# Keys in four loads, another order of the head, group 1's work between the first products, sums between the elu halves

## Chip, cores, metric

One core of one Trainium2 chip. The metric is device microseconds of the whole program. A "ratio" below is the mean time of one kernel's fast runs over that of the kernel before in the same rounds, with a 95% interval; it is not quite the ratio of the medians that are quoted beside it.

## The reference, cut

```python
# attention: batch 4, heads 4, seq 1088, head_dim 32, r 8
a, b = x @ S1.T, x @ S2.T                  # phi(x): outer product of a and b, 64 features
kv  = einsum('bhsf,bhsd->bhfd', phi(k), v);  z = sum(phi(k), seq)
x   = (phi(q) @ kv) / (phi(q) . z + 1e-6)  # -> (4352, 128)
# feed forward: w_in (128, 2048), w_out (2048, 128), both float64 in memory
h = x @ w_in;  g = where(h > 0, h, exp(min(h, 0)) - 1);  out = g @ w_out
```

## The kernel before, the parts that matter

Tokens go in 9 groups of 512 (the last of 256), d_ff in 8 pairs of 256 columns. A step is one pair of one group: `mm1` (two products h with w_in), `elu` (two ScalarE and one VectorE instruction for each half c, giving gg), and two steps later `mm2` (two products o with w_out, accumulated over a segment of pairs); `fin1` takes the accumulated o out of PSUM. Weights arrive as float64 and are rounded to fp32 on the chip, by `RA`, `RB` (ScalarE), `RC` (c, d, e), one pair at a time between about 10 and 60 us.

```python
    def round_e(raw, dst, pool=False):
        mant = raw[:, :, 0].bitcast(F32)
        if pool:                                   # pairs 4 to 7
            nc.gpsimd.tensor_mul(mant, mant, _ap(tiny[:], [[0, dst.shape[1]]]))
            nc.gpsimd.tensor_mul(dst, mant, dst)
        else:
            nc.vector.scalar_tensor_tensor(dst, mant, 2.0 ** -20, dst, op0=MUL, op1=MUL)
    ...
    load_hd(nc.sync, "k", k, 0, 0, KT)             # KT = 9 of 17 tiles of 32 floats: runs of 1152 bytes
    load_hd(nc.scalar, "k", k, 0, KT, NT)          # runs of 1024 bytes
    ...
    load_hd(nc.sync, "q", q, 0, 0, 8)
    load_w(0, 0);  load_v(nc.sync, 0);  load_w(1, 0);  load_w(1, 1);  load_w(0, 1)
    load_hd(nc.sync, "q", q, 0, 8, NT)
    ...                                            # the head (cut)
    keep_warm(2)                                   # filler products for TensorE
    transp(kT, "k", 0, 0, KT);  transp(kT, "k", 0, KT, NT)
    KF(0, 0);  transp(qT, "q", 0, 0, 8);  q1_first();  KO(0, 0);  KF(0, 1);  KF(0, 2);  q2_first()
    RA(0);  RB(0);  KO(0, 1);  KO(0, 2);  RA(1);  RA(2)
    KA(0, 0);  q4_first();  make_SX();  KA(0, 1);  RB(1);  RB(2);  KA(0, 2)
    transp(qT, "q", 0, 8, NT);  q5_first()
    mm1(0, 0)
    ...                                            # rounding of pair 1, then group 1: q2(1), mm1(0, 1), q4(1), q5(1)
    for n in range(N + 4):                         # the steps
        ...                                        # mm1, extras
        if 2 <= n < N:
            elu(g, cp)                             # both halves
        ...
        if 2 <= n < N + 2:
            mm2(...)
            if last:
                fin1(...)
```

KF makes the key features (abp), KO their outer product (kp), KA the products with v (kv), make_SX a small constant product (SX), q1 to q5 the same chain for the queries of a group.

## Time and profile before

| | |
|---|---|
| median (runs) | 303.12 us (302.9 to 303.38) |
| span of the profiled run | 300.9 us |
| busy: TensorE, VectorE, ScalarE, GpSimd | 96%, 56%, 62%, 6% |
| first product with w_in / products without holes / product o after the rounding | 20.19 / 28.41 / 63.61 us |

Shares of the whole span hide the stages: TensorE is nearly always full, so the questions are when the unbroken stream of h and o begins and which holes it has. The prediction shows the lines. In a timeline line the first number is the start in us, the second the length, and the bracket the idle time before it with its releaser.

### The profile page before, as it was taken

The page shows a single profiled execution, that of the slowest core. Times are in us where ns is not written, and L with a number is a line of the kernel's source. Part 1 is how long each engine was busy: PE and PEld are TensorE (multiplying, and loading weights), DVE is VectorE, ACT ScalarE, POOL GpSimd, SP SyncE. Part 2 cuts the span into 40 slices and gives each one's busy share as a digit, 9 for nine tenths or more (in the row PEclk, how much of TensorE's full clock was granted, in tenths as well). Part 3 has the DMA queues.
Part 4 walks back from the last instruction along what each step waited for, and adds up shares of the span by engine and source line. Part 5 has one row for each costly group of instructions (what it writes and reads, how often), then busy time and mean ns, then how long its engine had stood idle before and what let it go on. Part 6 is the DMA issues. An engine that isn't in the chain of part 4 may idle for free.

```text
span 300.9 us, 4049 instructions
## 1 busy us (share of the span) xinstructions
PE 290.1 (96%) x1454; PEld 147.7 (49%) x1454; DVE 169.7 (56%) x297; ACT 187.8 (62%) x354; POOL 17.1 (6%) x45
## 2 busy tenths in 40 slices
PE   8987999999999999999999999999999999999994
PEld 5863344644444455444544464445444444444682
DVE  5788899963745565536344656426443644354441
ACT  1526896565666645746775656656774687568682
POOL 2010023440000000100000000100000000000000
PEclk9999999999999999999999999999999999999999
DMA  6932998320010100001001100001001000110020
GB/s 187 338 118 74 200 216 201 48 74 0 9 28 9 27 2 0 2 9 27 2 1 17 18 2 0 0 14 23 0 0 23 16 0 1 15 22 0 3 33 17
DMA packets 38291, 13.37 MB, mean 44 GB/s; under 512 B 32768, under 2 KB 36480, under 8 KB 38272
## 3 DMA queue, kind: packets, MB, share of 16 engines
q1 hardware_dynamic: 37984, 12.86, 19.0%
q10 hardware_dynamic: 288, 0.26, 0.3%
q8 instruction: 11, 0.18, 0.2%
q14 instruction: 8, 0.07, 0.1%
HBM read 10.88 MB, written 2.23 MB: 44 GB/s over the span
## 4 chain that ended last, share of the span: by engine, by line
PE 83%; DVE 8%; ACT 3%; DMA 2%; issue 2%; SPq 1%; DVEq 0%
PE o L522 36%; PE h L493 34%; PE xps L472 3%; PE kv L293 3%; PE qtp L457 2%; PE abwp L360 2%; DMA v<-in_v_dram 2%; DVE gg L508 1%; ACT e L502 1%; PE abp L266 1%; ACT e L501 1%; DVE kT L247 1%; DVE kp L253 1%; DVE W L114 1%; PE x0ps L424 1%
## 5 line engine op out<-in xcount | busy, mean ns | idle before, releaser
L508 DVE SCALAR_TENSOR_TENSOR gg<-e,h 128x512 f32<-128x512 f32 (+1 forms) x144 | 93.0, 654 | 98.3 <-ACT e L502 97.8
L522 PE MATMUL o<-gg,W 128*128 128x512 f32 (+1 forms) x288 | 131.1, 578 | 1.2 <-ACT oT L535 0.7
L493 PE MATMUL h<-xg,W 128*128 128x512 f32 (+1 forms) x288 | 128.8, 569 | 1.8 <-DVE xg L484 0.7
L501 ACT ACTIVATE e<-h 128x512 f32<-128x512 f32 (+1 forms) x144 | 81.4, 565 | 26.1 <-PE h L493 25.7
L502 ACT ACTIVATE e<-e 128x512 f32<-128x512 f32 (+1 forms) x144 | 87.3, 606 | 4.6
L493 PEld LDWEIGHTS h<-xg,W 128*128 128x128 f32 x288 | 54.5, 190 | 65.2 <-issue 55.2
L522 PEld LDWEIGHTS o<-gg,W 128*128 128x128 f32 x288 | 51.9, 190 | 51.4 <-issue 43.7
L270 ACT COPY ab<-abp 128x256 f32<-128x256 f32 (+1 forms) x12 | 3.7, 317 | 25.0 <-PE abp L266 25.0
L365 ACT COPY abw<-abwp 128x384 f32<-128x384 f32 (+1 forms) x8 | 3.7, 458 | 22.9 <-PE abwp L360 22.9
L253 DVE TENSOR_TENSOR kp<-ab 128x1024 f32<-128x1024 f32 (+1 forms) x12 | 12.2, 1022 | 8.4 <-ACT ab L270 8.2
L458 ACT COPY qpT<-qtp 128x512 f32<-128x512 f32 (+1 forms) x16 | 8.3, 561 | 12.6 <-PE qtp L457 12.6
L293 PEld LDWEIGHTS kv<-v,kp 128*64 128x64 f32 (+1 forms) x288 | 9.5, 139 | 7.5 <-DVE gg L508 5.3
L293 PE MATMUL kv<-v,kp 128*64 128x33 f32 (+3 forms) x288 | 10.8, 226 | 0.3 <-DMA v<-in_v_dram 0.3
L381 DVE TENSOR_TENSOR qp<-an,abw 128x1024 f32<-128x1024 f32 (+1 forms) x8 | 9.3, 1159 | 0.3
L472 PE MATMUL xps<-qpT,kvS 64*32 64x128 f32 (+2 forms) x200 | 8.7, 298 | 0.3 <-ACT qpT L458 0.3
L483 ACT COPY xg<-xps 128x256 f32<-128x256 f32 (+1 forms) x8 | 2.9, 359 | 9.8 <-PE xps L472 9.8
L457 PEld LDWEIGHTS qtp<-ident,qp 128*128 128x128 f32 x60 | 6.8, 140 | 4.4 <-issue 4.0
L457 PE MATMUL qtp<-ident,qp 128*128 128x128 f32 x60 | 8.2, 277 | 0.6 <-DVE qp L381 0.6
L313 POOL TENSOR_TENSOR zm<-kvz,zmask 128x32 f32<-128x32 f32 x3 | 0.7, 241 | 126.0 <-ACT kvz L307 126.0
L266 PE MATMUL abp<-Sab,kT 128*64 128x64 f32 x136 | 7.4, 249 | 0.5 <-DVE kT L247 0.5
L360 PEld LDWEIGHTS abwp<-SW,qT 128*64 128x64 f32 x120 | 5.2, 136 | 5.4 <-issue 5.3
L266 PEld LDWEIGHTS abp<-Sab,kT 128*64 128x64 f32 x136 | 6.1, 159 | 3.6 <-issue 2.9
(84 smaller groups left out, 126.2 us busy)
## 6 DMA issues: line engine op xcount, KB each, us to landing
raw<-in_moe_w_in_dram SPq DMA_DIRECT2D x8, 256.0 KB, 5.7
raw<-in_moe_w_out_dram SPq DMA_DIRECT2D x8, 256.0 KB, 6.6
out_dram<-ob SPq DMA_DIRECT2D x104, 16.0 KB, 1.5
hd_k<-in_k_dram SPq DMA_DIRECT2D x3, 544.0 KB, 5.3
hd_q<-in_q_dram SPq DMA_DIRECT2D x3, 544.0 KB, 3.8
v<-in_v_dram SPq DMA_DIRECT2D x12, 72.0 KB, 5.3
v<-in_v_dram SPq DMA_DIRECT2D x12, 64.0 KB, 3.4
hd_k<-in_k_dram SPq DMA_DIRECT2D x1, 288.0 KB, 3.4
```

Source lines behind the costliest of these rows:

```text
L253: nc.vector.tensor_mul(dst, _ap(a_, list(a_.ap[1:]) + [[0, R]]), _ap(b_, [b_.ap[1], [0, R], b_.ap[2]]))
L266: nc.tensor.matmul(abp[64 * u:64 * u + 64, j * 64:j * 64 + 64], kT[b][:, u * KT + i, :], Sab[:].rearrange("p h y -> p (h y)"), skip_group_ ...
L293: nc.tensor.matmul(kv[64 * hp:64 * hp + 64, g2, :n], kp[:rows, j, h].rearrange("p i j -> p (i j)"), _ap(vt[b][:rows, off:off + D], [[VN - ...
L360: nc.tensor.matmul(p[64 * u:64 * u + 64, i * 96:i * 96 + 96], qT[b][:, t, :], SW[:, b].rearrange("p h x r -> p (h x r)"), skip_group_check ...
L381: nc.vector.tensor_mul(qp[g][:, :m], _ap(a_, list(a_.ap[1:]) + [[0, R]]), _ap(b_, [b_.ap[1], [0, R], b_.ap[2]]))
L457: nc.tensor.transpose(p[:, o:o + P], qp[g][:, r:r + 2].rearrange("p t i j -> p (t i j)"), ident[:])
L472: nc.tensor.matmul(xp[w][D * h:D * h + D, :nh * P].rearrange("p (m s) -> p m s", s=P)[:, m0:m0 + m, s], kvS[64 * w:64 * w + 64, b, h, :], ...
L493: nc.tensor.matmul(hs[g, cp][c][:, :n], W[:, cp, c * P:c * P + P], xg[g][:, :n])
L501: nc.scalar.activation(e, hs[g, cp][c][:, :n], RELU, scale=-1.0)
L502: nc.scalar.activation(e, e, EXP, scale=-1.0)
L508: nc.vector.scalar_tensor_tensor(gs[g, cp][:, c, :n], es[g, cp][:, c, :n], -1.0, hs[g, cp][c][:, :n], op0=ADD, op1=MAX)
L522: nc.tensor.matmul(ops[g][:, :n], W[:, cp, (2 + c) * P:(3 + c) * P], gg[:, c, :n], start=(first and c == 0), stop=(last and c == 1))
```

## The change

Its intent: let TensorE begin on a part of the keys; bring v before the weights; put the work that group 1 needs between the first two products; take GpSimd out of the rounding, where it and VectorE block each other; free the accumulator o half an elu earlier. The core of the diff (the mechanical parts are cut):

```diff
-    load_hd(nc.sync, "k", k, 0, 0, KT)
-    load_hd(nc.scalar, "k", k, 0, KT, NT)
+    KP = ((0, 4), (KT, KT + 4), (4, KT), (KT + 4, NT))
+    for i, t in enumerate(KP):
+        load_hd(nc.scalar if i % 2 else nc.sync, "k", k, 0, *t)
-    load_w(0, 0)
-    load_v(nc.sync, 0)
+    load_v(nc.sync, 0)
+    load_w(0, 0)
+    load_hd(nc.sync, "q", q, 0, 8, NT)
+    for t in KP[:2]:            # ahead of Sab on VectorE
+        transp(kT, "k", 0, *t)
-    keep_warm(2)
+    keep_warm(1)                # three later fillers in q5_first are gone too
+    for t in KP[2:]:
+        transp(kT, "k", 0, *t)
-    ... KA(0, 0); q4_first(); make_SX(); KA(0, 1); ... KA(0, 2); q5_first()
+    ... make_SX(); KO(0, 1); KO(0, 2); RA(0); RB(0); q2_first()
+    for i in range(3):
+        KA(0, i)
+    q4_first(); q5_first()
-    mm1(0, 0); (RC(1)); elu_a(0, 0, *); q2(1); mm1(0, 1); ... q4(1); ... q5_out(1, q5(1, True))
+    mm1(0, 0, (0,)); RA(1); RB(1); elu_a(0, 0, 0, (0,))
+    q2(1, 2); q4(1)             # outer product in two halves
+    mm1(0, 0, (1,)); elu_a(0, 0, 0, (1,)); RC(1)
+    x1 = q5(1, True); elu_a(0, 0, 1, (0,)); q5_out(1, x1); elu_a(0, 0, 1, (1,))
+    mm1(0, 1); ...
-        at(n, RC, i, i > 4)     # GpSimd for pairs 4 to 7
+        at(n, RC, i)
-            elu(g, cp)
+            elu(g, cp, 0)
+            if last: mm2(...); fin1(...)
+            elu(g, cp, 1)
```

More of the change, by code (lines that the diff above doesn't have):

```diff
@@ L93 @@
     nc.vector.memset(ebias[:], -float(896 << 23))
-    tiny = const.tile([P, 1], F32, name="tiny")
-    nc.gpsimd.memset(tiny[:], 2.0 ** -20)
     def round_a(raw, dst):
@@ L119, in round_d, with round_e @@
         nc.vector.scalar_tensor_tensor(lo.bitcast(F32), lo, 2.0 ** -32, raw[:, :, 1], op0=MUL, op1=ADD)
-    def round_e(raw, dst, pool=False):
-        mant = raw[:, :, 0].bitcast(F32)
-        if pool:
-            nc.gpsimd.tensor_mul(mant, mant, _ap(tiny[:], [[0, dst.shape[1]]]))
-            nc.gpsimd.tensor_mul(dst, mant, dst)
-        else:
-            nc.vector.scalar_tensor_tensor(dst, mant, 2.0 ** -20, dst, op0=MUL, op1=MUL)
+    def round_e(raw, dst):
+        nc.vector.scalar_tensor_tensor(dst, raw[:, :, 0].bitcast(F32), 2.0 ** -20, dst, op0=MUL, op1=MUL)
     S16 = const.tile([2 * R, D], F32, name="S16")
@@ L164, with round_w @@
     order = [(0, 1, 0), (1, 1, 1), (0, 0, 1)] + [(cp, 1, 1) for cp in range(2, NP)]
-    def round_w(f, i, *a):
+    def round_w(f, i):
         if wide:
@@ L169, in round_w @@
             c = slice(0 if w_in else 2 * P, 4 * P if w_out else 2 * P)
-            f(raw_w[cp][:, c], W[:, cp, c], *a)
+            f(raw_w[cp][:, c], W[:, cp, c])
     def RA(i):
@@ L176, in RB, with RC @@
         round_w(round_b, i)
-    def RC(i, pool=False):
+    def RC(i):
         round_w(round_c, i)
         round_w(round_d, i)
-        round_w(round_e, i, pool)
+        round_w(round_e, i)
+    load_v(nc.sync, 0)
     load_w(0, 0)
-    load_v(nc.sync, 0)
+    load_hd(nc.sync, "q", q, 0, 8, NT)
     load_w(1, 0)
@@ L187 @@
     load_w(0, 1)
-    load_hd(nc.sync, "q", q, 0, 8, NT)
     for cp in range(2, NP):
@@ L227, with transp @@
     nc.vector.tensor_copy(Sx[:], _ap(S16[:], [[0, H], [1, D]]))
+    def transp(dst, x, b, t0, t1):
+        nc.vector.transpose(dst[b][:, t0:t1, :].rearrange("p t (a c) -> p c t a", c=2), hd[x, b][:, :, t0:t1, :])
+    for t in KP[:2]:
+        transp(kT, "k", 0, *t)
     Sab = const.tile([FD, H, 2 * R], F32, name="Sab")
@@ L243, in make_SX @@
         nc.scalar.copy(SX[:], xps[:, :FD])
-    def transp(dst, x, b, t0, t1):
-        nc.vector.transpose(dst[b][:, t0:t1, :].rearrange("p t (a c) -> p c t a", c=2), hd[x, b][:, :, t0:t1, :])
     def outer(dst, ab):
@@ L312, in KZ1 @@
         z_ = kvz[b][:, :, :, D] if b == 0 else kvz[b][:, :, 0, D:]
-        (nc.vector if b == 0 else nc.gpsimd).tensor_mul(
+        nc.gpsimd.tensor_mul(
             zms[b][:], _ap(z_, [z_.ap[1], z_.ap[2] if b == 0 else [0, 2], [0, R]]),
@@ L366, in q1, with q2 @@
                        p[:, :n * 96].rearrange("p (t h y) -> p h t y", t=n, h=H))
-    def q2(g):
+    def q2(g, parts=1):
         m = H * qn[g]
@@ L378, in q2 @@
         qp[g] = work.tile([P, 4 * H, R, R], F32, name="qp", tag="qp", bufs=2)
-        a_ = an[:, :m]
-        b_ = x[:, :, :R]
-        nc.vector.tensor_mul(qp[g][:, :m], _ap(a_, list(a_.ap[1:]) + [[0, R]]),
-                             _ap(b_, [b_.ap[1], [0, R], b_.ap[2]]))
+        for i in range(parts):
+            h = slice(i * m // parts, (i + 1) * m // parts)
+            a_ = an[:, h]
+            b_ = x[:, h, :R]
+            nc.vector.tensor_mul(qp[g][:, h], _ap(a_, list(a_.ap[1:]) + [[0, R]]),
+                                 _ap(b_, [b_.ap[1], [0, R], b_.ap[2]]))
     def q1_first():
@@ L414, in q5_first @@
         KS(0)
-        round_w(round_c, 0)
-        round_w(round_d, 0)
-        keep_warm(2)
+        RC(0)
+        KZ2(0)
         xps = []
@@ L425, in q5_first @@
                                  kvz[0][:, g2].rearrange("p w d -> p (w d)"), skip_group_check=True)
-            if tt == 0:
-                KZ2(0)
-        round_w(round_e, 0)
-        q1(1)
-        keep_warm(1, P)
+        transp(qT, "q", 0, 8, NT)
         dn = work.tile([P, 2, 8], F32, name="dn", tag="dn", bufs=1)
@@ L437, in q5_first @@
             nc.vector.tensor_mul(xn[:, tt], xps[tt][:, :, :D], _ap(dn[:, tt], [[1, 8], [0, D]]))
-        xt = []
         for tt in range(2):
@@ L442, in q5_first @@
                 nc.tensor.transpose(q[:, t * P:t * P + P], xn[:, tt, 4 * t:4 * t + 4].rearrange("p m d -> p (m d)"), ident[:])
-            xt.append(q)
-        nc.scalar.copy(xg[0][:, :256], xt[0][:, :256])
-        nc.vector.tensor_copy(xg[0][:, 256:], xt[1][:, :256])
+            nc.scalar.copy(xg[0][:, 256 * tt:256 * tt + 256], q[:, :256])
+            if tt == 0:
+                q1(1)
     def q4(g):
@@ L487, with mm1, elu_a @@
     hs, es, gs, ops = {}, {}, {}, {}
-    def mm1(g, cp):
+    def mm1(g, cp, cs=(0, 1)):
         n = qn[g] * P
-        hs[g, cp] = [psum.tile([P, 512], F32, name="h", tag="h", bufs=4) for c in range(2)]
-        for c in range(2):
+        if 0 in cs:
+            hs[g, cp] = [psum.tile([P, 512], F32, name="h", tag="h", bufs=4) for c in range(2)]
+        for c in cs:
             nc.tensor.matmul(hs[g, cp][c][:, :n], W[:, cp, c * P:c * P + P], xg[g][:, :n])
-    def elu_a(g, cp, c):
+    def elu_a(g, cp, c, parts=(0, 1)):
         n = qn[g] * P
-        if c == 0:
+        if c == 0 and 0 in parts:
             es[g, cp] = work.tile([P, 2, 512], F32, name="e", tag="e", bufs=2)
         e = es[g, cp][:, c, :n]
-        nc.scalar.activation(e, hs[g, cp][c][:, :n], RELU, scale=-1.0)
-        nc.scalar.activation(e, e, EXP, scale=-1.0)
+        if 0 in parts:
+            nc.scalar.activation(e, hs[g, cp][c][:, :n], RELU, scale=-1.0)
+        if 1 in parts:
+            nc.scalar.activation(e, e, EXP, scale=-1.0)
     def elu_d(g, cp, c):
@@ L509, in elu_d, with elu @@
                                        op0=ADD, op1=MAX)
-    def elu(g, cp):
-        for c in range(2):
-            elu_a(g, cp, c)
-            elu_d(g, cp, c)
+    def elu(g, cp, c):
+        elu_a(g, cp, c)
+        elu_d(g, cp, c)
     def mm2(g, cp, first, last):
@@ L560, in fin2 @@
                 nc.sync.dma_start(rows[b, :, t:t + m, :], o[64 * u:64 * u + 64, i:i + m, :])
-    keep_warm(2)
-    transp(kT, "k", 0, 0, KT)
-    transp(kT, "k", 0, KT, NT)
+    keep_warm(1)
+    for t in KP[2:]:
+        transp(kT, "k", 0, *t)
     KF(0, 0)
     transp(qT, "q", 0, 0, 8)
-    q1_first()
     KO(0, 0)
     KF(0, 1)
+    q1_first()
     KF(0, 2)
-    q2_first()
+    make_SX()
+    KO(0, 1)
+    KO(0, 2)
     RA(0)
     RB(0)
-    KO(0, 1)
-    KO(0, 2)
-    RA(1)
-    RA(2)
-    KA(0, 0)
-    q4_first()
-    make_SX()
-    KA(0, 1)
-    RB(1)
-    RB(2)
-    KA(0, 2)
-    transp(qT, "q", 0, 8, NT)
-    q5_first()
-    mm1(0, 0)
-    round_w(round_c, 1)
-    round_w(round_d, 1)
-    round_w(round_e, 1)
-    for c in range(2):
-        elu_a(0, 0, c)
-    q2(1)
-    mm1(0, 1)
-    elu_a(0, 1, 0)
+    q2_first()
+    for i in range(3):
+        KA(0, i)
+    q4_first()
+    q5_first()
+    mm1(0, 0, (0,))
+    RA(1)
+    RB(1)
+    elu_a(0, 0, 0, (0,))
+    q2(1, 2)
+    q4(1)
+    mm1(0, 0, (1,))
+    elu_a(0, 0, 0, (1,))
+    RC(1)
+    x1 = q5(1, True)
+    elu_a(0, 0, 1, (0,))
+    q5_out(1, x1)
+    elu_a(0, 0, 1, (1,))
+    mm1(0, 1)
+    RA(2)
+    RB(2)
     for c in range(2):
         elu_d(0, 0, c)
-    q4(1)
-    round_w(round_c, 2)
-    q5_out(1, q5(1, True))
-    elu_a(0, 1, 1)
-    round_w(round_d, 2)
-    round_w(round_e, 2)
+    for c in range(2):
+        elu_a(0, 1, c)
+    RC(2)
+    RA(3)
     for c in range(2):
         elu_d(0, 1, c)
-    RA(3)
     RB(3)
@@ L657 @@
         if 2 <= n < N:
-            elu(g, cp)
+            elu(g, cp, 0)
+        if 2 <= n < N + 2:
+            g2, cp2, first, last = steps[n - 2]
+            if last:
+                mm2(g2, cp2, first, last)
+                fin1(g2, cp2 == NP - 1)
+                if cp2 == NP - 1 and g2 == NQ - 1:
+                    done[n + 2] = g2
+        if 2 <= n < N:
+            elu(g, cp, 1)
         for f, *a in extra.get((n, 1), ()):
             f(*a)
-        if 2 <= n < N + 2:
-            g, cp, first, last = steps[n - 2]
-            mm2(g, cp, first, last)
-            if last:
-                fin1(g, cp == NP - 1)
-                if cp == NP - 1 and g == NQ - 1:
-                    done[n + 2] = g
+        if 2 <= n < N + 2 and not last:
+            mm2(g2, cp2, first, last)
         if n in done:
```

## The prediction

> **What bounds the kernel now.** I read the page first, for busy shares and slices; then the timelines of TensorE and VectorE up to 64 us; then the chain of work that ended last; then the busy time of two stretches.
>
> ```profile
> PE 290.1 (96%) x1454; PEld 147.7 (49%) x1454; DVE 169.7 (56%) x297; ACT 187.8 (62%) x354; POOL 17.1 (6%) x45
> PE   8987999999999999999999999999999999999994
> DVE  5788899963745565536344656426443644354441
> ```
>
> TensorE is full in nearly every slice, so only two things can shorten this kernel: beginning the dense product stream earlier, and holes in it. VectorE is full in slices 4 to 8 only, about 30 to 60 us.
>
> ```profile
> 20.19 1.96 PE L493 MATMUL h<-xg,W 128*128 128x512 f32 x4 [0.61 <-DVE xg L445]
> 22.61 1.98 PE L493 MATMUL h<-xg,W 128*128 128x512 f32 x4 [0.47 <-DVE W L127]
> 25.18 1.07 PE L457 MATMUL qtp<-ident,qp 128*128 128x128 f32 x8 [0.59 <-DVE qp L381]
> 28.41 1.96 PE L493 MATMUL h<-xg,W 128*128 128x512 f32 x4 [0.68 <-DVE xg L484]
> 30.20 1.88 PE L522 MATMUL o<-gg,W 128*128 128x512 f32 x4
> ```
>
> TensorE's timeline: the first product with w_in starts at 20.19, but each step up to 28.41 waits for VectorE. Only from 28.41 do products follow each other, at 1.72 us per pair (32.08 to 33.80 in the chain).
>
> ```profile
> 28.40:63.60 35.20, 34.00 (x174) 15.96 (x174) 33.59 (x54) 26.40 (x48) 10.49 (x8) 1.00 0.72 147
> 63.60:301.00 237.40, 232.35 (x1060) 114.95 (x1060) 115.30 (x190) 149.77 (x284) 3.33 (x15) 1.00 0.07 12
> ```
>
> Busy us by stretch, in the order PE, PEld, DVE, ACT, POOL. From 28.4 to 63.6 TensorE (34.00 of 35.20) and VectorE (33.59) are both full: this is where w_in and w_out are rounded. After 63.6 TensorE alone is the bound; its missing 5 us there are mostly the tail. So an earlier start is worth no more than VectorE can follow up to 63.6, where the chain runs through VectorE:
>
> ```profile
> 60.56 1.23 DVE qT L247
> 61.79 1.17 DVE gg L508 x2
> 62.95 0.61 DVE oT L531
> 63.61 1.98 PE o L522 x4
> ```
>
> **What the Trainium skill says.** (1) "SBUF — State Buffer", section "Who interferes with whom": a VectorE instruction with two SBUF inputs contends with a GpSimd instruction that reads SBUF, as an exclusive lock, and the loser blocks fully. The trace agrees:
>
> ```profile
> 44.01 1.30 POOL L125 TENSOR_TENSOR W<-raw,W 128x512 f32<-128x512 f32 x1
> 44.13 1.72 DVE L114 SCALAR_TENSOR_TENSOR W<-raw,W 128x512 uint32<-128x512 uint32 x1
> 55.01 1.15 POOL L124 TENSOR_TENSOR raw<-raw,tiny 128x512 f32<-128x512 f32 x1 [5.46 <-DVE raw L119]
> 55.18 2.06 DVE L253 TENSOR_TENSOR kp<-ab 128x1024 f32<-128x1024 f32 x1
> ```
>
> L114 normally takes 0.69 and kp 1.22; each ends about 0.55 and 1.1 after the POOL instruction that started just before it. That costs VectorE 1.03 + 0.84 = 1.9 us. (2) "GPSIMD Engine Reference", "3.1 Elementwise — side-by-side cycle accounting": an elementwise op of two tensors is 1.96 times slower there. Here 1.30 against 0.69 us, 1.9 times. (3) "DMA: Bandwidth & Descriptors", "Issuing engines are not separate DMA queues": transfers of all issuers share the 16 engines. So splitting the keys brings bandwidth nothing; it can only change what lands first. In the trace the load share is full from 5 to 15 us. (4) "TensorE: Matmul & The Clock Gate", "What's actually happening": it runs at half clock until some 3.4 us of activity. The first fillers of 256 columns take about 1 us each, those at 14.67 0.53, so it is warm by then. The change leaves no TensorE hole over 1.3 us, so I charge nothing for the fillers removed.
>
> **The change, part by part.** I walk the new order through with the durations of the old trace, starting each instruction at the later of its input and its engine's last end, plus the 0.15 us that the trace shows from a VectorE or ScalarE end to TensorE's start.
>
> *Keys.* All 544 KB had landed by about 5.4, from about 3.1: 240 KB/us. The first two quarters (256 KB) should land at about 4.3, so two transposes of about 0.4 end at 5.1, before Sab (then 5.3 instead of 5.14). With the filler ending at 5.8, the first key products begin at 5.8 instead of 6.81: 1.0 gained. Queries land as before (6.1 to 6.4). kp's three parts end at 8.5, 9.65 and 10.0 instead of 9.6 to 12.4.
>
> *v ahead of w_in.* v has 256 KB fewer ahead of it, at about 350 KB/us 0.7 us: 9.3 instead of 10.03. The first w_in lands where v did, 10.0. RA(0) stands before the query outer product, which then runs 10.2 to 11.4 (0.7 later than before). The 36 kv products take 1.29 + 1.46 = 2.75: 9.4 to 12.2 instead of 14.7. Here lies the head's gain.
>
> *Then* kvz to 12.6; zm on POOL 0.24, with kvS behind it (1.4, wanted only at 21); q transposes 12.2 to 13.1, their copies to 13.95; wps, x0ps to 15.2. VectorE: RC(0) 1.6 to 14.2, SW 0.15, qT 0.7 to 15.05, dn and xn 2 x 0.77 to 16.6, RA(1) 0.4. x0tp, q1(1), x0tp, then xg at 18.0. **First product 18.15, against 20.19.**
>
> *Group 1 between the first products.* abw at 17.7, den chain 1.34, qp in halves to 19.7 and 20.35; transposes at 19.85 and 20.5; qpT to 21.7; q5 at 21.9 to 23.1. RC(1), 2.5 us, on VectorE 20.35 to 22.85, beside all of this, where before it stood ahead of q2(1). mm1(0,1) 23.1 to 24.85, then mm1(1,0) without a hole. **Dense from 24.85 instead of 28.41: 3.55.** The first product with w_out waits for RC(2), whose end I get at 26.55: 26.7 against 30.36, 3.7.
>
> *VectorE to the end of the rounding.* RC(3) starts at 28.1 (gg(0,1) ends then) against 31.38: 3.28. From here VectorE has no hole. Added: four round_e from POOL, about 0.65 net each, 2.6. Removed: the 1.9 of blocking, and the 0.6 since the sum (L531) now stands before the second elu half, so the o buffer is free one gg earlier. Step by step: kT at 44.15 (46.96 before), RC(7) at 50.0 (53.05), the second qT at 58.05 (60.56), sum done at 60.5. **So the product o at 63.61 moves to about 60.6: 3.0.** TensorE could be there at 24.85 + 34.0 = 58.9; it loses the 1.7 in waiting for the key transpose and the sum.
>
> *After that* nothing is removed from TensorE. At the ends of groups the earlier copy saves a few tenths at most: all waits for oT L535 and L531 together are 1.2 us of TensorE, and they lie at 37.9, 63.6 and once later. I take 0.1. The fewer fillers lie in waits.
>
> Sum: 303.12 - 3.0 - 0.1 = **300.0 us**.
>
> **Rivals.** (a) *VectorE takes it all back.* If round_e costs 2.6 and the blocking was not additive (a later wait absorbs it), 63.61 moves by about 1.2 only: 301.9. For it: VectorE is at 95% in that stretch. Against: the two long instructions lie in a stretch without VectorE holes. (b) *TensorE is the bound there, not VectorE*: then all 3.6 and 1.2 of holes come through, 298.3. For it: TensorE shows 34.00 busy of 35.20. Against: the chain at 63.61. (c) *The first w_in or the small key pieces land late.* RA(0) blocks VectorE's queue, so each us late moves the head by one; 1 us gives 301, as the dense part has some slack against VectorE. The pieces have 512-byte runs instead of 1152. (d) *The moved sum delays gg.* VectorE now waits for the product with w_out before the second gg half. By the old distances that half is wanted about 2.5 us after it, so nothing; if it does stall at each of 9 groups by 0.3, 302.5.
>
> **Range and chances.** The ends of (a) and (b) with some room for (c): 298.1 to 301.9. Over 2% faster needs 297.06, 6 us, which no path gives, since the dense products alone end only 3.6 earlier: 0.05. Over 2% slower needs rival (d) doubled with no gain in the head: 0.01. Within 2%: 0.94.
>
> **What would show it.** Right: kv products at 9.4 ending 12.2; first h at about 18.2; unbroken h and o from about 24.9; first o at 26.7; L114 and kp without long cases and POOL empty after 15 us; a wait of o or of the keys' abp on VectorE between 43 and 61; o after the second qT at about 60.6; stretches after it equally long. Wrong: kv waiting beyond 10 for v, RA(0) waiting past 10.3 for w_in, VectorE ending the second qT beyond 61, or new TensorE waits at group ends after 64 us.

## The result, and the profile after

The changed kernel took 302.99 us (302.08 to 303.16, 4 runs) against 303.25: ratio 0.9987, interval 0.9965 to 1.0009. The same. A gain of 3.1 us had been forecast. The profiled run is the fastest of the four (302.08, span 300.3). Executions over 1.5% slower than the fastest of the same kernel are left out of the means.

TensorE's timeline of the kernel after, to be read against the one in the prediction:

```profile
10.69 0.76 PE L242 MATMUL SXps<-Sx,idr 8*128 8x128 f32 x2 [0.47 <-ACT ab L266]
11.38 3.70 PE L289 MATMUL kv<-v,kp 128*64 128x64 f32 x72
20.86 1.13 PE L486 MATMUL h<-xg,W 128*128 128x512 f32 x2 [0.48 <-ACT xg L435]
25.80 3.70 PE L486 MATMUL h<-xg,W 128*128 128x512 f32 x8 [0.37 <-DVE W L120]
29.34 1.88 PE L516 MATMUL o<-gg,W 128*128 128x512 f32 x4
48.15 0.69 PE L262 MATMUL abp<-Sab,kT 128*64 128x64 f32 x16 [1.31 <-DVE kT L224]
62.91 1.98 PE L516 MATMUL o<-gg,W 128*128 128x512 f32 x4
```

The first product with w_in comes 0.7 us later than before, not 2.0 earlier. From then on the change works: from the first product to the first o it takes 8.5 us (10.0 before), so that the first o is 0.9 us ahead, and the o after the rounding still 0.7. From there both kernels take the same 237.4 and 237.3 us. So all that is missing went before 20.86. Two things differ there. The first, in VectorE's timeline after and before, is the key transposes:

```profile
4.05 0.75 DVE L224 STREAM_TRANSPOSE kT<-hd_k 128x256 f32<-128x256 f32 x2
6.81 0.51 DVE L224 STREAM_TRANSPOSE kT<-hd_k 128x320 f32<-128x320 f32 x1 [1.71 <-DMA hd_k<-in_k_dram]
7.67 0.45 DVE L224 STREAM_TRANSPOSE kT<-hd_k 128x256 f32<-128x256 f32 x1 [0.34 <-DMA hd_k<-in_k_dram]
```

```profile
5.05 1.36 DVE L247 STREAM_TRANSPOSE kT<-hd_k 128x576 f32<-128x576 f32 x2
```

The first half of the keys is transposed a microsecond earlier, but the whole is ready at 8.1 instead of 6.4 us. The chain that ended last now runs through the fourth piece, 128 KB on ScalarE's queue (start, length):

```profile
2.01 5.63 DMA hd_k<-in_k_dram
7.67 0.46 DVE kT L224
```

The second is the length of the kv products. The 72 of them took 3.70 us; before they took 1.29 and 1.53 us in two parts. The view of the tile kv gives the shortest, median and longest record in ns, after and before:

```profile
L289 PE MATMUL kv<-v,kp x72: 218/314/368, 11.4 to 14.9; 128*64 128x64 f32 x64, 64*64 64x64 f32 x8
```

```profile
L293 PE MATMUL kv<-v,kp x72: 218/222/368, 10.2 to 14.5; 128*64 128x64 f32 x64, 64*64 64x64 f32 x8
```

The same instruction, with all its inputs there, has a median of 314 instead of 222 ns. The Trainium skill ("TensorE: Matmul & The Clock Gate", "What's actually happening") has the clock at half until a window of some 3.4 us is busy. I call this TensorE cold. The granted clock in the profile doesn't show it: it reads 1.00 from 11 to 15 us in both kernels. So it had to be tested; a profile in which the clock does show is that of e6, below.

### The profile page after: what moved, and what is told of

The parts are those of the page before. It is cut to its first block, busy times and chain, and to the rows that moved or that the text cites. A ratio compares the mean times of both kernels' runs of the same rounds, so it can differ in the third digit from the quotient of the medians.

```text
span 300.3 us, 4026 instructions
## 1 busy us (share of the span) xinstructions
PE 289.1 (96%) x1446; PEld 147.2 (49%) x1446; DVE 170.0 (57%) x302; ACT 187.8 (63%) x355; POOL 7.1 (2%) x37
## 4 chain that ended last, share of the span: by engine, by line
PE 75%; DVE 9%; DMA 5%; SPq 4%; ACT 2%; issue 2%; ACTq 0%; DVEq 0%
PE o L516 33%; PE h L486 30%; DMA v<-in_v_dram 4%; SPq L88 3%; PE kv L289 3%; PE xps L464 2%; PE abwp L356 2%; PE qtp L449 2%; DMA hd_k<-in_k_dram 2%; DVE kT L224 1%; DVE gg L503 1%; PE abp L262 1%; ACT e L497 1%; DVE raw L117 1%; SPq L76 1%
## 5 line engine op out<-in xcount | busy, mean ns | idle before, releaser
L249 DVE TENSOR_TENSOR kp<-ab 128x1024 f32<-128x1024 f32 (+1 forms) x12 | 11.2, 949 | 7.0 <-ACT ab L266 6.8
L289 PEld LDWEIGHTS kv<-v,kp 128*64 128x64 f32 (+1 forms) x288 | 10.5, 153 | 7.1 <-DVE gg L503 4.5
L289 PE MATMUL kv<-v,kp 128*64 128x33 f32 (+3 forms) x288 | 11.7, 240 | 0.0
L262 PE MATMUL abp<-Sab,kT 128*64 128x64 f32 x136 | 8.1, 250 | 2.5 <-DVE kT L224 2.5
L464 PEld LDWEIGHTS xps<-qpT,kvS 64*32 64x32 f32 x200 | 4.2, 105 | 5.5 <-ACT e L497 3.8
```

What stands on the lines that cost most here:

```text
L249: nc.vector.tensor_mul(dst, _ap(a_, list(a_.ap[1:]) + [[0, R]]), _ap(b_, [b_.ap[1], [0, R], b_.ap[2]]))
L262: nc.tensor.matmul(abp[64 * u:64 * u + 64, j * 64:j * 64 + 64], kT[b][:, u * KT + i, :], Sab[:].rearrange("p h y -> p (h y)"), skip_group_ ...
L289: nc.tensor.matmul(kv[64 * hp:64 * hp + 64, g2, :n], kp[:rows, j, h].rearrange("p i j -> p (i j)"), _ap(vt[b][:rows, off:off + D], [[VN - ...
L464: nc.tensor.matmul(xp[w][D * h:D * h + D, :nh * P].rearrange("p (m s) -> p m s", s=P)[:, m0:m0 + m, s], kvS[64 * w:64 * w + 64, b, h, :], ...
```

## The experiments

Theory A: the four small key loads land late, and the head hangs on the last. Theory B: fewer fillers and more holes leave TensorE cold in the kv products. Rival to both: the stretch to 63 us is bound by VectorE's work, and the head is beside the point. The runs were made on three chips; the kernel before ran beside each group, with medians of 303.36, 303.08, 303.07 and 303.0 us, so times of different groups can be compared to some tenths.

### First four: loads and fillers

**e1_two_loads**: the changed kernel with two key loads.

```diff
-    KP = ((0, 4), (KT, KT + 4), (4, KT), (KT + 4, NT))
+    KP = ((0, KT), (KT, NT))
-    for t in KP[:2]:      # the two transposes ahead of Sab: none; all follow keep_warm(1)
```

> The changed kernel with the keys of group 0 in two loads again (as before), all key transposes after Sab; everything else as changed. Theory A (the four small key loads land late and hold the head): the last key transpose ends near 6.6 us instead of 8.1, the second key products run near 7.7 instead of 8.2 to 9.2, the kv products start near 9.8 (when v is there) instead of 11.4, the first product with w_in starts near 19.2 instead of 20.9, and the time falls by about 1.5 us against the changed kernel (ratio to the kernel before about 0.994). Rival B (a cold TensorE in the kv products is what costs): they still take 3.7 us, the first product moves by less than 0.6 us and the time by less than 0.5.

Measured: 299.23 us (298.68 to 299.48, 6 runs), ratio 0.9855 (0.9822 to 0.9889): 3.8 us under the changed kernel, two and a half times the expectation. TensorE's timeline:

```profile
10.24 2.46 PE L289 MATMUL kv<-v,kp 128*64 128x64 f32 x72
18.48 1.12 PE L486 MATMUL h<-xg,W 128*128 128x512 f32 x2 [0.49 <-ACT xg L435]
```

kv starts 1.14 us earlier and takes 1.24 less: in this execution A and B went away together. I put the second down to the fewer holes of TensorE with the keys there, which e1 alone doesn't show. The first product, predicted at 18.15 for the changed kernel, is at 18.48. The rival to both falls: e1 takes next to no work off VectorE, and yet the o after the rounding comes at 60.35 instead of 62.91 us.

**e2_fillers**: the changed kernel with `keep_warm(1)` after the first key products and `keep_warm(1, P)` before SX.

> The changed kernel with two fillers more on TensorE in its early holes (one of 256 columns after the first key products, one of 128 before SX). Rival B (cold TensorE): the 72 kv records take about 2.8 us instead of 3.7, the first product starts near 20.0 instead of 20.9, the time falls by about 0.9 us against the changed kernel. Theory A alone: the late keys still hold kv at about 11.4, the kv products stay near 3.7 us, and nothing is gained.

Measured: 300.89 us (300.03 to 303.9), ratio 0.9936. The profiled run:

```profile
11.72 2.46 PE L289 MATMUL kv<-v,kp 128*64 128x64 f32 x72
19.96 1.12 PE L486 MATMUL h<-xg,W 128*128 128x512 f32 x2 [0.48 <-ACT xg L435]
```

The last key transpose was even later here (8.41 us), kv starts later, and yet the first product is at 19.96 instead of 20.86. So B is real by itself, worth 1.24 us in kv and 0.9 at the first product. Two of the six runs were at 303.65 and 303.9, so that fillers don't help every time while the keys are late.

**e3_two_loads_fillers**: both.

> Two key loads and two more fillers at once. If A and B both count: kv from about 9.8 to 12.6, first product with w_in near 18.4, rounding of pair 2 (RC(3)) starts near 28.3 instead of 30.7, time about 300.6 us, ratio to before about 0.991. If only A counts, as e1 within 0.3 us; if only B, as e2.

Measured: 299.38 us (298.3 to 299.87), ratio 0.9859. No better than e1, whose six runs lie within 0.8 us and whose profile is warm: the second filler even pushed kv from 10.24 to 10.74. The 300.6 that I expected was too cautious, and the two effects don't add where one removes the other.

**e4_before_split**: the kernel before with its two key loads cut in four, nothing else.

> The kernel before with nothing but its two key loads split in four. Theory A: the key transposes end near 8.1 instead of 6.4, the first key products start near 8.3 instead of 6.8, kv starts near 11.2 instead of 10.2, and the time rises by about 0.8 us. If the small loads cost nothing that matters (hidden behind v), the kv start stays at 10.2 and the time within 0.3 us of before.

Measured: 304.81 us (304.3 to 307.96), ratio 1.0055 (1.0011 to 1.0099): 1.4 us slower by the medians (0.8 expected). Its key transposes end at 7.9 us and kv starts at 11.3 instead of 10.2. A holds in the other direction, without any other part of the change.

### Why the small loads are late

**e5_four_full_runs**: e1 with each load cut by the parity c instead of by tiles: four pieces on the same two queues, with runs of 1152 and 1024 bytes instead of 512 and 640.

```diff
-    for i, t in enumerate(KP):
-        load_hd(nc.scalar if i % 2 else nc.sync, "k", k, 0, *t)
+    for c in range(2):
+        for i, t in enumerate(KP):
+            load_hd(nc.scalar if i % 2 else nc.sync, "k", k, 0, *t, slice(c, c + 1))
```

> As e1_two_loads, but its two key loads cut in four by the parity c, so that each piece still moves runs of 1152 or 1024 bytes (the changed kernel's pieces have runs of 512 and 640). Theory A1 (the short runs make the keys slow): the last key transpose ends near 6.5 us, kv starts near 10.3, time within 0.4 us of e1 (299.2). Rival A2 (the second piece on ScalarE's queue, issued late and sharing with the queries and v behind it, is what is slow, whatever its runs): the last transpose ends near 7.7 to 8.2, kv near 11, time near 301 or more.

**e6_four_one_queue**: the changed kernel with all four pieces on SyncE.

```diff
-        load_hd(nc.scalar if i % 2 else nc.sync, "k", k, 0, *t)
+        load_hd(nc.sync, "k", k, 0, *t)
```

> The changed kernel with its four key pieces all issued by SyncE in one queue, ahead of the queries. Theory A2 (sharing with the other queue): the last piece lands by about 6.2 us, since nothing is ahead of it, its transpose ends near 6.7, kv starts near 10.3 or, as everything behind is issued 1.3 us later, near 10.7; time near 300. Theory A1 (short runs): the last piece still lands near 7.6 and kv starts at 11.4 or later; time 303 or more.

Measured: e5 299.8 us (299.16 to 301.79), its keys transposed by 6.3 us; e6 302.89 us (301.99 to 303.98), its last key transpose at 6.45, but the queries only there at 9.09:

```profile
9.09 0.71 DVE L224 STREAM_TRANSPOSE qT<-hd_q 128x512 f32<-128x512 f32 x1 [2.20 <-DMA hd_q<-in_q_dram]
```

Neither of my two explanations is the whole. In e6 the last piece lands 3.2 us after its issue, so short runs alone don't hold it; in e5 a second piece on ScalarE's queue lands within 2.9, so that queue alone doesn't either. What decides is seen in the stretch from 2 to 8 us, last column GB/s, in the order before, changed, e1, e5, e6:

```profile
2.00:8.00 6.00, 5.82 (x33) 3.99 (x34) 3.58 (x13) 1.51 (x3) 0.86 (x6) 1.00 0.89 255
```

```profile
2.00:8.00 6.00, 5.33 (x27) 3.34 (x26) 3.20 (x14) 1.86 (x3) 0.87 (x6) 1.00 0.89 222
```

```profile
2.00:8.00 6.00, 5.95 (x42) 4.10 (x43) 3.81 (x14) 1.86 (x3) 0.87 (x6) 1.00 0.91 251
```

```profile
2.00:8.00 6.00, 5.84 (x40) 4.01 (x40) 3.12 (x13) 1.86 (x3) 0.86 (x6) 1.00 0.96 249
```

```profile
2.00:8.00 6.00, 4.90 (x41) 3.19 (x40) 3.31 (x14) 1.54 (x4) 0.86 (x6) 1.00 0.81 188
```

With runs of 1024 bytes and more the core receives 249 to 255 GB/s here, whether in two pieces or four; with 512 and 640 it receives 222 and 188 (in e6 later issues from one queue are in that number too). The other profiles keep to this: 237 to 264 with long runs, 208 to 227 with short ones. By my reading the loss is paid by whoever is behind: the fourth key piece where it shares with the queries and v of the other queue, the queries where they stand behind the keys. In e5 too the queries came later than in e1 (7.8 against 6.8 us), which I don't explain; its profiled run was a cold one.

The profile of e6 also shows the clock itself. The granted clock reads 0.50 for 3.4 us, from 11.4 to 14.8, some time after a hole of 2.33 us in TensorE; in it the kv products run at the pace of the changed kernel's (median 314 ns in both). The kv products in half a microsecond of e6, the changed kernel and e1 (PE's busy time, with their number in brackets; the granted clock is the third number from the right):

```profile
12.50:13.00 0.50, 0.50 (x15) 0.50 (x13) 0.00 (x0) 0.00 (x0) 0.50 1.09 354
```

```profile
12.50:13.00 0.50, 0.50 (x14) 0.50 (x14) 0.00 (x0) 0.00 (x0) 1.00 1.08 363
```

```profile
10.50:11.00 0.50, 0.50 (x26) 0.50 (x22) 0.00 (x0) 0.00 (x0) 1.00 1.08 365
```

So the slow kv products are what half clock looks like, and the reading of 1.00 in the changed kernel's profile is not to be trusted there; why it reads so is not shown. e4's profile, too, reads 0.50 for 3.4 us (7.6 to 11.0) after a hole of 1.77 us.

### The other parts of the change, one by one

These stand on e1, so that the late keys don't hide them.

**e7_pool_round**: the last rounding step of pairs 4 to 7 back on GpSimd (`at(n, RC, i, i > 4)` and the code of before).

> e1_two_loads with the last step of the rounding of pairs 4 to 7 back on GpSimd, as in the kernel before. The prediction's sum says that this removal cost VectorE 2.6 and saved 1.9 us; by the two traces the stretch from RC(3) to the second query transpose went from 29.2 to 29.7. So: the key transpose of batch 1 starts about 0.4 us earlier than in e1 (44.14), and the time is 0.3 to 0.5 us lower than e1. Rival: the blocking by GpSimd costs more than it saves; time above e1 by 0.5 or more.

Measured: 299.22 us (298.85 to 301.07), against e1's 299.23. The key transpose of the next batch came at 43.77 instead of 44.14, as expected, but the 0.3 to 0.5 us that I expected of it did not come: this part of the change costs or gains nothing measurable.

**e8_old_sums**: `fin1` after both elu halves, as before.

> e1_two_loads with the sums copied after both elu halves, as in the kernel before. Prediction: VectorE's sum ends 0.6 us later at about 60.8, TensorE's product o at 60.35 moves to about 60.9, and the copy on ScalarE makes TensorE wait about 0.6 us once more near 35; as the wait for the key transpose at 45 absorbs the second of these, the time rises by 0.5 to 0.7 us against e1. Rival: the sums' place changes nothing, since TensorE comes as late by itself: within 0.2 us.

Measured: 300.27 us (299.95 to 302.56), about 1 us over e1 and e7 (three of its four runs at 299.95 to 300.33; 0.5 to 0.7 was expected). Its profile fell on the fourth, which is cold. TensorE waits again there where the changed kernel does not:

```profile
63.41 1.98 PE L516 MATMUL o<-gg,W 128*128 128x512 f32 x4 [1.15 <-DVE oT L525]
```

**e9_old_group1**: the first two products, the rounding of pair 1 and their elu ahead of group 1's work, as before (the order is that of the kernel before from `mm1(0, 0)` to `RB(3)`, with RA and RB of pairs 1 and 2 just behind the first product).

> e1_two_loads with the middle of the head as in the kernel before: both first products, the rounding of pair 1 and their elu before group 1's den chain, transposes and products. By the traces, from the first product with w_in to the start of RC(3) the old order takes 11.2 us and the new 9.7: so RC(3) starts about 1.5 us later than in e1 (28.1) and the time rises by about 1.3 us, to 300.6. Rival: the stretch up to 60 us is bound by VectorE's total work, which the order doesn't change, so that the time stays within 0.4 us of e1.

Measured: 301.01 us in the median of the five fast runs (300.69 to 301.79), ratio 0.9936. The profiled execution was broken (756.7 us, TensorE slow all through), so its trace says nothing.

**e12_w_before_v**: `load_w(0, 0)` ahead of `load_v` again.

> e1_two_loads with the first load of w_in ahead of v again, as before. The prediction counted the order of v and w_in as the head's gain (v 0.7 us earlier lets kv start at 9.4). In e1 kv starts at 10.24 behind SX, not behind v, which lands by about 9.3. So with v 0.7 us later kv starts at 10.1 to 10.3 and the time is within 0.3 us of e1. Rival (the prediction): kv 0.7 us later, time up by 0.7.

Measured: 300.27 us (299.07 to 301.17), in two kinds: 299.07, 299.14, 299.5 and 301.04, 301.15, 301.17. The profile fell on the second kind: kv starts at 10.36 right behind SX, not waiting for v, and takes 3.99 us. So the order of v and w_in moves nothing measurable here. The gap of 1.5 to 2.1 us between the two kinds I take for TensorE cold or warm; only the cold kind has a profile here, but of e1 there are both (e14, below).

### How often it is cold, and what group 1's place gave

**e13_changed_again**, **e14_two_loads_again** and **e15_old_group1_again** are the changed kernel, e1 and e9 unaltered, on one chip in the same rounds.

> The changed kernel, unaltered, six more executions beside the next three. Its profile had the kv products at 3.70 us (cold TensorE). If that is its rule, all executions lie between 302 and 303.3 us and the new profile has kv at 3.6 to 4.0 us again; if cold and warm executions alternate, some lie 1.2 to 1.9 us lower, near 301.

> e1_two_loads, unaltered, on the chip of the next one: about 299.2 us in warm executions (kv 2.46 us), with perhaps some near 301 (cold).

> e9_old_group1, unaltered, whose profile fell on a broken execution. In a good profile RC(3) starts 1.5 us later after the first product than in e14 (11.2 instead of 9.7 us) and the time is 1.3 to 2 us above e14's. If it is within 0.4 us, the place of group 1's work does not matter.

| run | executions, us | kv start and length in the profiled one |
|---|---|---|
| e13, changed | 302.5, 302.69, 302.84, 303.34, 303.62, 303.7 | 12.03, 4.30 (303.7) |
| e14, two loads | 298.38, 298.92 and 301.04, 301.1, 301.11, 301.16 | 10.56, 3.90 (301.16) |
| e15, old group 1 | 300.61, 300.73, 300.76, 301.01, 301.77, 303.38 | 10.26, 2.46 (301.77) |

```profile
12.03 4.30 PE L289 MATMUL kv<-v,kp 128*64 128x64 f32 x72
```

The changed kernel has one kind of execution, up to 0.4 us slower here than the 303.3 that I allowed, and both of its profiles are cold. e14 has two kinds about 2.4 us apart. The same kernel has a warm profile in e1 and a cold one here: the first product is at 18.48 and at 20.24, and the executions took 299.3 and 301.16, so that nearly the whole difference arises in the head. In e15, whose profile is warm, TensorE waits again between the first products for the rounding of pair 1:

```profile
18.49 1.99 PE L486 MATMUL h<-xg,W 128*128 128x512 f32 x4 [0.48 <-ACT xg L435]
21.76 1.98 PE L486 MATMUL h<-xg,W 128*128 128x512 f32 x4 [1.28 <-DVE W L120]
```

Two warm profiles with the same head are the cleanest comparison: in e1 and e15 the first product starts at 18.48 and 18.49, but RC(3) at 28.14 and 30.53, and the executions took 299.3 and 301.77. Within one chip, from the first product to RC(3) it takes 12.0 us in e15 and 9.7 in e14. So group 1's place is worth about 2.4 us, more than the 1.3 to 2 that I expected. The medians, 300.88 and 301.07, would have hidden it, because four of e14's six are of the slower kind; which of e15's other executions were warm is not shown.

### A version that beats both

In e1 TensorE still waits for the key transpose of the next batch, and VectorE's sum is ready just when TensorE wants it. TensorE's timeline of e1:

```profile
45.59 0.69 PE L262 MATMUL abp<-Sab,kT 128*64 128x64 f32 x16 [1.29 <-DVE kT L224]
60.35 1.98 PE L516 MATMUL o<-gg,W 128*128 128x512 f32 x4
```

**e10_moved_transposes**: the key transpose ahead of the rounding in its step, the query transpose a step later.

```diff
-        at(n, transp, kT, "k", b, 0, NT)
+        extra.setdefault(n, []).insert(0, (transp, kT, "k", b, 0, NT))
-        at(n + 3, transp, qT, "q", b, 0, NT)
+        at(n + 4, transp, qT, "q", b, 0, NT)
```

> e1_two_loads with the key transpose of the next batch ahead of the rounding in its step and the query transpose one step later. In e1 TensorE waits 1.29 us for the key transpose at 45 us, then runs dense up to the product o at 60.35, where VectorE's sum is ready at 60.23. If both engines bind there, moving 1.3 us of VectorE work behind the sum and the transpose forward lets TensorE pass without the wait: o near 59.1, time near 298.0 (1.2 less than e1). If VectorE's total binds in another place (elu halves of steps 6 to 9), the gain is under 0.4 us.

Measured: 298.06 us (297.93 to 300.03), ratio 0.9844. As expected, with kv at 10.04:

```profile
44.04 0.69 PE L262 MATMUL abp<-Sab,kT 128*64 128x64 f32 x16
58.98 1.98 PE L516 MATMUL o<-gg,W 128*128 128x512 f32 x4
```

**e11_moved_pool**: e10 with the GpSimd rounding of e7.

> e10 with the last rounding step of pairs 4 to 7 on GpSimd as well. If TensorE alone binds in e10, the same time within 0.3 us (about 298.0); if VectorE still binds there, 0.3 to 0.6 us less than e10; if the blocking by GpSimd hurts, more than e10.

Measured: 298.78 us (297.97 to 299.07), not better than e10. With GpSimd back two kp instructions of its trace take 2.32 and 2.08 us instead of 1.22, and TensorE waits 0.46 us for one of them at 53.31 (0.22 in e10).

**e16_moved_fillers**: e10 with `keep_warm(2)` before the key products and `keep_warm(1, P)` before SX.

> e10_moved_transposes with two fillers more (256 columns before the key products, 128 before SX). If the spread between executions is TensorE's cold head, all executions lie within 0.6 us of each other at about 298.0 to 298.6 and kv takes 2.46 us; if not, some lie near 300 still.

Measured: 298.01 us (297.24 to 298.34, 4 runs), ratio 0.9827 (0.9808 to 0.9846). All four lie within 1.1 us, more than the 0.6 expected but without a second kind 2 us apart; kv takes 2.46 us in the profile. By the medians this is the best of the kernels here, 5 us under both, though not distinguishable from e10.

## Why the prediction was wrong, step by step

The sum failed in one place, the head up to the end of the kv products: predicted 12.2 us, measured 15.1. Of these 2.9 us, 2.0 lie in the start of the kv products (11.38 against 9.4), of which e1 takes back 1.1, and 0.95 in their length. Behind it the steps held, each by its own length (predicted, then measured in the profile after):

| step of the prediction | predicted | measured |
|---|---|---|
| kv end to first product with w_in | 6.0 | 5.8 |
| first product to mm1(1,0) | 6.7 | 6.7 |
| first product to RC(3) | 9.95 | 9.83 |
| RC(3) to the sum done | 32.4 | 32.2 |
| stretch behind it against before | equal | 237.4 against 237.3 |

- **"Keys": failed.** The first half was in time (4.05 against 4.3). But I took one rate, 240 KB/us, for runs of 1152 bytes, used it for runs of 512 and 640, and let the second half and the queries land as before. The second half was transposed by 8.1 instead of about 6, and the transpose of the queries began at 8.04 instead of about 6.4. Shown by e1 (kv 1.1 us earlier) and e4 (the split alone makes the kernel before 1.4 us slower). Rival (c) names the run length, but allows one microsecond and lets slack absorb it.
- **"I charge nothing for the fillers removed": failed.** I reasoned that no hole exceeds 1.3 us, and took TensorE's warmth at 14.67 in the trace before for granted in the new order. No hole in the head was longer than 0.8 us in the profile after, and TensorE was cold all the same: the 72 kv products took 3.70 us where I had 2.75, and 4.30 in a second profile. Shown by e2 (fillers alone: 2.46) and by e6, whose granted clock reads 0.50 in such products.
- **"v ahead of w_in ... here lies the head's gain": wrong cause.** kv does not wait for v in any of the changed orders, but stands behind SX, which stands behind the last key products. e12 shows the order of the loads to be worth nothing measurable.
- **"Group 1 between the first products": right** in mechanism; the 1.5 us or so that my sum gives it (3.55 less 2.0) was about 2.4 (e1, e14, e15).
- **"VectorE to the end of the rounding": right in sum.** GpSimd's part nets to nothing (e7), the sums give about 1 instead of 0.6 (e8). That both engines bind up to 63 us, and that TensorE loses its wait at the key transpose, came as said: 1.31 us at 48.15. Removing that wait took work off VectorE's queue before the sum at the same time (e10).
- **The range** 298.1 to 301.9 did not contain 302.99. With the keys left in two loads the kernel runs at 299.2 when warm and 301.1 when cold, so the estimate of everything else was sound in its sum.

One reading of the prediction is loose: VectorE's row of slices shows 8 or 9 from slice 3 to slice 8, 15 to 60 us, and not from about 30 us only. No sum rests on it.

What stays open: why TensorE is warm in some executions of e1 and cold in others at nearly the same instruction times (the page named in the list below has a reason, which no run here tests), why the granted clock reads 1.00 in most of the cold profiles, and why e5's queries were late.

## What to carry to other kernels

Before cutting a load so that work can begin on its first part, look at the length of its runs and at what stands behind it: the first part came a microsecond earlier, the last 1.7 us later, and the chain hung on the last. Cut along an axis that keeps the runs whole. Fillers that only seem to fill waits can be what keeps TensorE warm; compare the records' ns of the same instruction before and after, not only the holes. And when a change bundles several parts, undo one at a time: here two parts, group 1's place and the sums, are worth about 2.4 and 1 us, and the cut keys, with the cold TensorE of the new head, took it all.

## What the Trainium skill lacked or had wrong

- "DMA: Bandwidth & Descriptors", "Specifications", gives 512 bytes as the smallest transfer for line rate. Here loads in runs of 512 and 640 bytes took the core's rate from 2 to 8 us from 237 to 264 GB/s (all profiles with long runs) down to 208 to 227, and to 188 where all went through one queue. Other loads are in these rates, so they are no clean test of the line rate.
- The same page, "Issuing engines are not separate DMA queues", says that the queues interleave, but not what this does to a small load behind another: 128 KB in 512-byte runs, second on ScalarE's queue, landed after 5.63 us; the same piece last in SyncE's queue after 3.2; pieces of that size in runs of 1024 bytes, on the same two queues, within 2.9.
- "TensorE: Matmul & The Clock Gate", "What's actually happening", says that the cold part varies from run to run, as the window runs free of the kernel, and costs under 1%. The runs agree in size: one kernel had executions 2.4 us, 0.8%, apart. To be added: the granted clock is no sure sign of it. It read 1.00 through the slow kv products of the profile after and 0.50 through those of e6, and the records' lengths told both times (64 columns: median 314 ns in both, 222 in the profile before).
- "SBUF — State Buffer", "Who interferes with whom", and the GpSimd ratio cited in the prediction held. But GpSimd's help and its blocking nearly cancelled: 299.22 us with it, 299.23 without.
